# Gated linear attention and a SoLU feed-forward: preparation in groups of two batches, weights converted by VectorE, second product one chunk later

One Trainium2 chip, one core. The metric is the device time of the kernel in microseconds (us), the median of several executions. All executions compared here are fast: none lies more than 1.5% above the fastest of its kernel. The "granted clock" is the share of TensorE's full clock that the profile shows as granted, 1 for all of it. Engines: TensorE (PE in the profile), VectorE (DVE), ScalarE (ACT), GpSimd (POOL).

## The reference, cut to what matters

```python
# q, k, v, a_re, a_im: (4 batches, 8 heads, 768 steps, 48)
mag = np.sqrt(a_re * a_re + a_im * a_im)
scale = np.minimum(mag, 0.999) / (mag + 1e-06)          # then a_re, a_im times scale
for t in range(S):                                      # complex state S, decayed by a
    new_re = ar * S_re - ai * S_im
    new_im = ar * S_im + ai * S_re
    S_re, S_im = (new_re + k[t] (x) v[t], new_im)
    y[t] = q[t] @ S_re
x = y as (3072, 384)
h = x @ w_in                                            # 384 x 1024
e = np.exp(h - h_max); solu = h * e / (sum(e) + 1e-9)
ln = (solu - mu) / np.sqrt(var + 1e-06) * g_ln
return ln @ w_out                                       # 1024 x 384
```

The weights w_in and w_out and the vector g_ln arrive in 64-bit floating point.

## The kernel before

A chunk is 128 steps of one batch; there are 24, in 6 rows of 4 batches. For a row, `prep_steps` computes the logarithm of the decay, its running sum (a matmul with a triangle), and sine and cosine of the summed angle. From these k and q are scaled, "doubled" to a real and an imaginary part, and turned (transposed) by TensorE. Then come the scores, the values and the state of the attention, and for the chunk before it the feed-forward: turn of x, `up` (two halves of 512 columns), exp and product (`solu`), turn of z, `down`.

VectorE, ScalarE and TensorE execute in exactly the order in which the loop emits their work; the loop is therefore a schedule for three queues. It prepares the next row of four batches during four passes (`part` 0 to 3):

```python
    for n in range(N + 1):
        ...                                        # cut: loads; part = b, now = the next row's preparation
        if n > 0:
            turn_x()                               # feed-forward of chunk n-1
        if n < N:
            score(0); score(1)
        if last_ff:
            last_ff[6]()                           # store of chunk n-2
        if part == 0:   now["s0"]()
        elif part == 1: now["s3"]()
        elif part == 2: now["decay"]()
        elif part == 3: now["trig"](); to_exp()
        if nxt:
            doubled(*nxt)
        if n > 0:
            up(0); solu(0); up(1)
        if part == 3:
            now["ends"]()
        if nxt:
            turn("k", *nxt, 0); turn("q", *nxt, 0)
        if n > 0:
            solu(1)
        if n < N:
            values()
        if n > 0:
            turn_z(0); turn_z(1)
        if n < N:
            carry()
        if nxt:
            turn("k", *nxt, 1); turn("q", *nxt, 1)
        ...                                        # cut: weights in passes 0 and 1
        if part == 1:
            now["s4"]()
        if n > 0:
            down(0); norm()
        if part == 0:
            now["s1"](); now["s2"]()
        elif part == 1:
            run(now["totals"])
        elif part == 2:
            to_trig(); now["angle"]()
        if n > 0:
            down(1)
        if part == 2:
            run(now["phases"])
```

The weights are made 32-bit floats by integer operations in 14 pieces. Each piece alternates between VectorE and GpSimd:

```python
    # ScalarE: y = the low word, rounded
    ts(out=x, in0=hi, scalar1=0x7FFFFFFF, scalar2=None, op0=OP.bitwise_and)
    nc.gpsimd.tensor_tensor(out=x, in0=x, in1=rebias.to_broadcast([P, n]), op=OP.add)
    ts(out=hi, in0=hi, scalar1=-2 ** 31, scalar2=None, op0=OP.bitwise_and)
    stt(out=x, in0=x, scalar=31, in1=x, op0=OP.arith_shift_right, op1=OP.bitwise_and)
    stt(out=x, in0=x, scalar=3, in1=hi, op0=OP.logical_shift_left, op1=OP.bitwise_or)
    nc.gpsimd.tensor_tensor(out=w[:, c, f0:f0 + n].bitcast(I32), in0=x, in1=y, op=OP.add)
```

The steps of the preparation that the argument needs, with the engine of each: `s0`, `s1` (VectorE, ScalarE: Ln, Exp, the ratio of the parts), `s2` (ScalarE: squares and Ln), `s3` (VectorE, then ScalarE's Exp and Ln), `s4` (VectorE), `totals` (TensorE, with the tile f_L), `decay` (ScalarE: two Exp), `ends` (TensorE turns the chunk's last decays, tile f_tot), `angle`, `phases` (TensorE, tile f_phase), `trig` (ScalarE: two Sin). All turned tiles, f_L, f_tot and f_phase share one pool of two banks of PSUM, the memory that TensorE writes to here: a matmul waits until the tile before it in its bank has been read.

## Time and profile before

| Measure | Before |
|---|---|
| Time, median of 4 runs (lowest to highest) | 634.35 us (634.05 to 635.15) |
| Profiled span, mean granted clock | 635.8 us, 0.902 |
| TensorE busy | 498.8 us (78%) |
| Turn of x of pass n=2 begins | 158.11 us |
| Turn of x of n=2 to that of n=22 | 423.4 us |

The last two rows are read from the timeline of TensorE; they divide the span into a start, twenty passes and an end.

### The profile page before, as it was taken

To read this page: it belongs to the slowest core of one execution; us is meant where nothing else is said; L and a number is where in the kernel's file an instruction comes from. 1 tells how busy PE (TensorE), PEld (TensorE's weight loads), DVE (VectorE), ACT (ScalarE), POOL (GpSimd) and SP (SyncE) were. 2 spreads that over 40 slices of the span, in tenths; PEclk is the share of its full clock that TensorE was granted. 3 is DMA by queue.
4 is the path that set the end of the run, shared out by engine and by line. 5 is a ranking of instruction groups with operands and counts; after the bars stand their busy time and mean duration, and the time that the engine had idled before them with its cause. 6 is when DMAs were issued, how large, how long until landed. Compare 5 with 4: busy or idle time off the path is not lost.

```text
span 635.8 us, 12921 instructions
## 1 busy us (share of the span) xinstructions
PE 498.8 (78%) x5600; PEld 316.5 (50%) x5600; DVE 343.1 (54%) x565; ACT 282.7 (44%) x428; POOL 164.8 (26%) x159
## 2 busy tenths in 40 slices
PE   0334060287989889999799897999997999999994
PEld 0113050154646656556466465565664765666652
DVE  3674656615665655646646556556465465444232
ACT  2665343450653553644526535536345356223221
POOL 1072545200600515303216005152031160000000
PEclk9955565597999989999799999899997999999998
DMA  9949411000383001950004830019500000000000
GB/s 179 222 96 194 124 50 50 2 1 0 74 153 63 3 13 26 148 104 14 13 2 83 142 64 12 4 27 159 92 14 12 2 15 14 13 14 14 13 14 19
DMA packets 132019, 35.94 MB, mean 57 GB/s; under 512 B 126960, under 2 KB 130032, under 8 KB 131952
## 3 DMA queue, kind: packets, MB, share of 16 engines
q1 hardware_dynamic: 131312, 34.62, 27.8%
q8 instruction: 46, 0.75, 0.5%
q10 hardware_dynamic: 640, 0.40, 0.3%
q14 instruction: 21, 0.17, 0.1%
HBM read 30.22 MB, written 4.72 MB: 55 GB/s over the span
## 4 chain that ended last, share of the span: by engine, by line
PE 58%; ACT 14%; DVE 13%; POOL 6%; issue 4%; SPq 2%; DMA 0%; DVEq 0%; ACTq 0%; POOLq 0%
PE f_h L867 18%; PE f_o L909 13%; PE f_turned L799 6%; PE f_score L815 5%; PE f_zt L884 3%; PE f_d L842 3%; PE f_y L827 2%; PE f_L L708 2%; DVE f_bits L631 2%; SPq L584 2%; PE f_phase L758 2%; PE f_y L830 2%; POOL f_rs L903 2%; ACT f_kT L801 1%; DVE f_x L746 1%
## 5 line engine op out<-in xcount | busy, mean ns | idle before, releaser
L867 PE MATMUL f_h<-f_w_in,f_xT 128*128 128x512 f32 x288 | 140.4, 641 | 45.7 <-ACT f_xT L862 45.7
L909 PE MATMUL f_o<-f_w_out,f_zT 128*128 128x384 f32 x384 | 131.8, 495 | 4.2 <-DVE f_w_out L644 3.9
L867 PEld LDWEIGHTS f_h<-f_w_in,f_xT 128*128 128x128 f32 x288 | 57.2, 206 | 112.0 <-issue 95.7
L909 PEld LDWEIGHTS f_o<-f_w_out,f_zT 128*128 128x128 f32 x384 | 72.1, 193 | 50.4 <-DVE f_w_out L644 4.5
L876 DVE TENSOR_TENSOR f_z<-f_h,f_z 128x512 f32<-128x512 f32 x48 | 33.1, 690 | 88.6 <-ACT f_z L875 88.6
L817 DVE TENSOR_TENSOR f_att<-f_score,f_mats 128x512 f32<-128x512 f32 x48 | 32.8, 689 | 68.9 <-PE f_score L815 68.9
L801 ACT COPY f_kT<-f_turned 96x512 f32<-96x512 f32 x48 | 27.8, 580 | 62.5 <-PE f_turned L799 62.2
L846 POOL TENSOR_TENSOR f_state<-f_state,f_tot 96x384 f32<-96x384 f32 x16 | 19.0, 1187 | 134.9 <-DVE f_state L845 134.9
L862 ACT COPY f_xT<-f_xt 128x384 f32<-128x384 f32 x24 | 11.4, 474 | 94.6 <-PE f_xt L859 94.6
L799 PE MATMUL f_turned<-f_mats,f_k 128*96 128x128 f32 x192 | 31.8, 291 | 26.2 <-DVE f_k L787 25.5
L815 PE MATMUL f_score<-f_qT,f_kT 96*128 96x128 f32 x384 | 49.3, 284 | 0.0
L902 POOL TENSOR_TENSOR f_s<-f_s,f_mv 128x1 f32<-128x1 f32 x24 | 10.3, 431 | 142.3 <-DVE f_s L901 142.3
L815 PEld LDWEIGHTS f_score<-f_qT,f_kT 96*128 96x128 f32 x384 | 47.2, 200 | 0.0
L875 ACT ACTIVATE f_z<-f_h 128x512 f32<-128x512 f32 x48 | 28.8, 599 | 30.7 <-PE f_h L867 30.6
L723 POOL TENSOR_TENSOR f_q<-f_q,f_ar 128x384 f32<-128x384 f32 x22 | 29.1, 1351 | 50.6 <-ACT f_ar L715 50.6
L799 PEld LDWEIGHTS f_turned<-f_mats,f_k 128*96 128x96 f32 x192 | 21.2, 131 | 40.1 <-issue 26.8
L708 PE MATMUL f_L<-f_lr,f_mats 128*128 128x384 f32 x48 | 20.3, 554 | 25.6 <-DVE f_lr L701 25.5
L885 ACT COPY f_zT<-f_zt 128x512 f32<-128x512 f32 x48 | 27.7, 586 | 22.4 <-PE f_zt L884 22.0
L884 PE MATMUL f_zt<-f_mats,f_z 128*128 128x128 f32 x192 | 29.9, 286 | 6.0 <-DVE f_z L876 6.0
L827 PE MATMUL f_y<-f_v,f_att 128*32 128x48 f32 x1536 | 34.4, 210 | 0.0
L758 PE MATMUL f_phase<-f_x,f_mats 128*128 128x384 f32 x48 | 22.3, 582 | 15.3 <-ACT f_x L743 7.2
L827 PEld LDWEIGHTS f_y<-f_v,f_att 128*32 128x32 f32 x1536 | 30.9, 112 | 5.1 <-issue 4.9
(100 smaller groups left out, 821.4 us busy)
## 6 DMA issues: line engine op xcount, KB each, us to landing
f_ar<-in_a_re_dram SPq DMA_DIRECT2D x24, 192.0 KB, 4.4
f_ai<-in_a_im_dram SPq DMA_DIRECT2D x24, 192.0 KB, 4.6
f_q<-in_q_dram SPq DMA_DIRECT2D x24, 192.0 KB, 4.7
f_k<-in_k_dram SPq DMA_DIRECT2D x24, 192.0 KB, 4.3
f_v<-in_v_dram SPq DMA_DIRECT2D x24, 192.0 KB, 4.3
out_dram<-f_ot SPq DMA_DIRECT2D x24, 192.0 KB, 1.9
f_raw<-in_moe_w_in_dram SPq DMA_DIRECT2D x6, 512.0 KB, 6.1
f_raw<-in_moe_w_out_dram SPq DMA_DIRECT2D x8, 384.0 KB, 3.1
```

Source lines behind the costliest of these rows:

```text
L708: nc.tensor.matmul(out=ps, lhsT=tri, rhs=lm, start=True, stop=True)
L723: el.tensor_tensor(out=x, in0=x, in1=t[:, o], op=OP.mult)
L758: nc.tensor.matmul(out=ps, lhsT=turns, rhs=T["x0", ti][:, b * DM:(b + 1) * DM], start=True, stop=True)
L799: nc.tensor.transpose(out=ps[0:D2, i], in_=T[nm + "2", ti, b][:, half * 4 + i].rearrange("p u d -> p (u d)"), identity=ident)
L801: nc.scalar.copy(out=T[nm + "T", ti, b][:, half * 512:half * 512 + 512], in_=ps[0:D2].rearrange("p i t -> p (i t)"))
L815: nc.tensor.matmul(out=ps[:, i], lhsT=KT[:, x * P:(x + 1) * P], rhs=QT[:, x * P:(x + 1) * P], start=True, stop=True)
L817: nc.vector.tensor_tensor(out=st["att"][:, half * 4:half * 4 + 4], in0=ps, in1=tri.unsqueeze(1).to_broadcast([P, 4, P]), op=OP.mult)
L827: nc.tensor.matmul(out=y[g:g + 32, hs], lhsT=st["att"][:, x, g:g + 32], rhs=V[:, hs], start=True, stop=(ti == 0))
L867: nc.tensor.matmul(out=h, lhsT=st["xT"][:, c * P:(c + 1) * P], rhs=w_in[:, c, half * 512:(half + 1) * 512], start=(c == 0), stop=(c == KD ...
L876: nc.vector.tensor_tensor(out=z, in0=h, in1=z, op=OP.mult)
L884: nc.tensor.transpose(out=ps[:, i * P:(i + 1) * P], in_=st["z"][:, c * P:(c + 1) * P], identity=ident)
L909: nc.tensor.matmul(out=st["o"], lhsT=st["zT"][:, c * P:(c + 1) * P], rhs=w_out[:, c], start=(c == 0), stop=(c == KF - 1))
```

## The change

Its intent: shorten the start, in which TensorE has nothing to do, by preparing two batches (a group) instead of four and by taking the weights off GpSimd; and keep GpSimd, slower at elementwise work in this trace (1187 ns against 554 for 96x384, see the prediction), out of the loop. The second product (`down`) of a chunk moves one pass later. A test that no weight is too small for the shorter conversion is added (each piece is fetched again later). The weights, now three operations in one queue:

```diff
-    # six operations, VectorE and GpSimd in turn
+    nc.vector.tensor_scalar(out=x, in0=hi, scalar1=3, scalar2=0x3FFFFFFF, op0=OP.logical_shift_left,
+                            op1=OP.bitwise_and)
+    nc.vector.scalar_tensor_tensor(out=x, in0=hi, scalar=-2 ** 30, in1=x, op0=OP.bitwise_and,
+                                   op1=OP.bitwise_or)
+    nc.vector.tensor_tensor(out=x, in0=x, in1=T["bits", i], op=OP.add)
+
+    def inspect(i):
+        nc.vector.tensor_reduce(out=least[:, i:i + 1], in_=T["raw", i][:, :, 1].bitcast(FP), axis=AX.X, op=OP.min,
+                                apply_absolute_value=True)
```

Groups, pools and the engine of the elementwise work (cut):

```diff
-    const, ld, ldv = pool("f_const", 1), pool("f_ld", 1), pool("f_ldv", 2)
+    const, ld, ldv = pool("f_const", 1), pool("f_ld", 2), pool("f_ldv", 3)
-    rawp = pool("f_raw", 4)
+    rawp, bits = pool("f_raw", 6), pool("f_bits", 3)
-    groups = [(0, 0, 2), (0, 2, B)] + [(ti, 0, B) for ti in range(1, NC)]
+    GB = 2
-            nc.gpsimd.tensor_scalar(out=ai, in0=ai, scalar1=1e15, scalar2=-1e15, op0=OP.min, op1=OP.max)
+            nc.vector.tensor_scalar(out=ai, in0=ai, scalar1=1e15, scalar2=-1e15, op0=OP.min, op1=OP.max)
-                nc.gpsimd.tensor_tensor(out=heads(state[b]), in0=heads(state[b]), in1=tot, op=OP.mult)
+                nc.vector.tensor_tensor(out=heads(state[b]), in0=heads(state[b]), in1=tot, op=OP.mult)
```

The new loop prepares a group in two passes, an even and an odd one (a pair). Conditions are shortened: `even` and `odd` hold only while there is a group to prepare.

```diff
+    for n in range(N + 2):
+        ...                                       # cut: loads, fetches, `if` around work that is not there
+        store of chunk n-3
+        turn_x()                                  # feed-forward of chunk n-1
+        score(0); score(1)
+        if even: now["s1"]()
+        if odd:  now["trig"](); to_exp(); now["decay"]()
+        down(0)                                   # of chunk n-2
+        if even: doubled(nxt)
+        values()
+        if even: now["square"]()
+        up(0); solu(0)
+        if even: now["s2"]()
+        if odd:  now["decayed"](0); doubled(nxt); now["decayed"](1)
+        turn("k", nxt, 0); turn("q", nxt, 0)
+        up(1); solu(1)
+        if even: now["s3"]()
+        if odd:  now["ends"]()
+        carry()
+        turn("k", nxt, 1); turn("q", nxt, 1)
+        if even: now["s4"]()
+        if odd:  then["s0"]()
+        turn_z(0)
+        if even: now["totals"](); now["fourth"](); to_trig(); now["angle"]()
+        down(1)
+        turn_z(1); norm()
+        if 4 <= n < 18: inspect(n - 4)
+        if even: now["phases"]()
```

## The prediction

> **What bounds the kernel now.** I read the page's busy rows first, then the chain that ended last in order of time, then the timelines of single stretches.
>
> ```profile
> PE 498.8 (78%) x5600; PEld 316.5 (50%) x5600; DVE 343.1 (54%) x565; ACT 282.7 (44%) x428; POOL 164.8 (26%) x159
> ...
> PE   0334060287989889999799897999997999999994
> ...
> POOL 1072545200600515303216005152031160000000
> PEclk9955565597999989999799999899997999999998
> ```
>
> TensorE is the bound from the tenth slice on (each is 15.9 us), but not before: up to about 158 us it is mostly idle. So there are two stretches to price: the start, and 22 to 24 chunks in which TensorE is nearly full.
>
> The start hangs on GpSimd. Each piece of weights goes VectorE, GpSimd, VectorE, GpSimd, one piece after the other:
>
> ```profile
> 103.69 0.99 POOL L633 TENSOR_TENSOR f_w_out<-f_bits 128x384 int32<-128x384 int32 x1 [1.15 <-DVE f_bits L632]
> 105.15 1.00 POOL L625 TENSOR_TENSOR f_bits<-f_bits,f_rebias 128x384 int32<-128x384 int32 x1 [0.47 <-DVE f_bits L624]
> 107.30 0.99 POOL L633 TENSOR_TENSOR f_w_out<-f_bits 128x384 int32<-128x384 int32 x1 [1.16 <-DVE f_bits L632]
> ```
>
> That is 3.6 us a piece until 111 us. The first product of a chunk's second part starts at 122.9 us, the centring of the weights ends at 147 us, and the third pass of the loop (call it n=2) starts at 158.1 us.
>
> In the steady stretch one row of four chunks takes 86.6 us (the preparation's first maximum starts at 203.13, 289.70 and 377.38 us in the chain). The last chunks, which prepare nothing, run full:
>
> ```profile
> 564.68 1.79 PE f_score L815 x16
> 566.47 5.15 PE f_h L867 x12
> 575.28 1.27 PE f_turned L799 x8
> 576.55 5.16 PE f_o L909 x16
> 582.04 1.79 PE f_score L815 x16
> ```
>
> One such chunk takes 17.36 us, of which I count 16.9 as work (0.33 turn x, 1.78 score, 5.16 up, 4 x 0.43 turn k and q, 1.55 values, 1.1 turn z, 5.16 down). A row with preparation has 4 x 16.9, 4 x 0.85 for the carry and 8 x 0.65 + 0.15 for the sums and phases: 76.4 us. So only 10 us of 86.6 are waits and their slow clock, nearly all in one place:
>
> ```profile
> 219.05 1.48 ACT L689 ACTIVATE f_ar<-f_x 128x1536 f32<-128x1536 f32 x1 [5.13 <-POOL f_rs L903]
> ...
> 223.70 0.46 ACT L862 COPY f_xT<-f_xt 128x384 f32<-128x384 f32 x1
> ```
>
> ScalarE's queue holds the copy of x behind a Square that waits for VectorE. TensorE waits there, and the products behind it take 7.1 to 8.4 us in the chain instead of 5.15.
>
> **What the Trainium skill says.** "TensorE: Matmul & The Clock Gate", section "Architectural detail", has ScalarE and VectorE as strict FIFOs; the trace agrees (the turn of x began at 218.25 us, and its copy above came at 223.70, behind work that it does not need). The same page, "What's actually happening", lets the clock fall after an idle window of about 3.4 us; the page's PEclk of 5 to 6 tenths in the slices with an idle TensorE agrees. "GPSIMD Engine Reference", section "Engine selection", puts two-input elementwise work at about twice VectorE's time there; the trace has 1187 ns against 554 for 96x384. "ScalarE: Activation LUTs", section "What ACT_TABLE_LOAD costs", states 1283 ns plus a drain of 1380: the trace has the 1283 ns, and the next activation starts 0.01 us later, so I charge no drain.
>
> **The change, part by part.** Weights: 14 pieces, each now two ScalarE operations (0.76+0.72 us for 512 columns, 0.64+0.61 for 384) and three on VectorE (about 0.43+0.69 and an integer add, which the trace lacks; I take 0.65 to 1.1). GpSimd's 34 us there go. Preparing two batches instead of four halves the first chain. I walked the queues by these durations: loads land at 6 us as now, phases at 22, sums at 27, Sin at 32, first turned halves at 36, so the loop begins near 38 us, not 78. Pass n=0 converts six pieces; the last four go raise, convert, scale at 2.5 us each, and the pass ends near 70. Pass n=1 has four more at 2.5, then the mean (5.4) and the centring, ending near 115. So n=2 starts at 115 against 158: 43 us won. Of this 5 us is owed, since the second product of chunk 0 is still to do.
>
> GpSimd's work on VectorE: per two chunks 0.5+0.96 for the imaginary part, 4 x 0.55 for k and q, 2 x 0.55 for the state: about 5 us, to about 32 us of VectorE in some 39 us of TensorE. That fits as a share. What matters is where it stands. The queues of a pair of chunks in the changed kernel (read from the built order) give four waits for TensorE:
> - Odd pass: k and q are decayed behind the first half's exp and product, then doubled, then turned, while the second half of "up" stands behind the turn. From the end of up(0): 0.2+0.72 exp, 0.61 product, 2 x 0.47, 0.95 doubling, 0.05: 3.5 us, plus 0.4 for q.
> - Odd pass: the transpose of the end values comes behind the second product: 0.2+0.72+0.69+0.54+0.1 = 2.25 us, plus 0.45 later for a bank.
> - Even pass: the transpose of z needs a PSUM bank of the turned k, whose copy stands behind s3's Exp and Ln, which wait for VectorE's s3 behind the second product: 0.2+0.72+0.61+0.95+0.9+0.93+0.6 = 5.0, less 1.7 of carry and turns that run beside it: 3.3 us, plus 0.5 at sums and phases.
> - Odd turn of x: its bank is freed by the phase's subtraction, behind the angle's row and the statistics: about 1.6 us.
>
> Together 12 us per pair. Work per pair is 2 x 16.9 + 1.7 + 2.8 = 38.3, so about 50 us per pair, 25 per chunk, against 86.6/4 = 21.65 before. The wait at the Square goes (it is in the sum: the copy of x now stands ahead of it), but four smaller ones come in every pair instead of one in two pairs.
>
> Second product a chunk later: it removes most of the half microsecond by which a full chunk is longer than its work (17.36 against 16.9) and adds a pass at the end, where it fills gaps: about +3 us net. Table loads: 27 instead of 13, 18 us more on ScalarE at 1.283 each, mostly beside TensorE. Weights fetched again for the test of smallness: 5.6 MB and about 7 us of VectorE over 14 passes, hidden apart from 0.6 per even pass, which is in the 1.6.
>
> Sum: 115 + ten pairs n=2 to 21 (first and last shorter) 497 + n=22 and 23 16.8+15.1 + end 25 = 669 us of span, 667 as timed. Since each wait could be some tenths shorter, I put 660.
>
> **The rivals.** First, TensorE stays full: without the new waits the ten pairs cost about 383 us plus little, and the sum is near 560. For it speaks that the total busy time fits and that the change moves so much off the slow engine; against it, that the waits above are chains inside strict queues, which more buffers do not shorten. Second, only the bare chains count: with the smallest latencies the waits sum to 9.6 us, a pair costs 48, the start ends at 105, and the time is about 635 to 640: the start's gain eaten whole. Third, the waits of 3.3 to 3.5 us drop the clock as the one of 3.7 us does now; with 1 us per pair for it the time is near 680. I hold the main sum the likeliest, since the same counting gives 76 + 10 for a row of the kernel before.
>
> **Range and chances.** Ten pairs carry the uncertainty: 1 us per pair is 10 us. A pair of 47.5 to 51.5 us and a start of 107 to 120 give 632 to 684. Faster than 621 needs pairs under 46 us, which asks that two of the four waits are not there: 0.12. Within 2% (622 to 647) is the second rival: 0.2. Slower: 0.68.
>
> **What would show it.** Right: n=2's turn of x near 115 us; waits of TensorE for the doubled k (3.5 us, 11 times), for the end values' transpose (2 us), for the copies of the turned k before z's transpose (3 us); a pair near 50 us; a busy share of TensorE near or below 75%; GpSimd nearly empty. Wrong: pairs near 40 us in the chain, or an integer add on VectorE of several us, which would lengthen the start.

## More of the kernel before

The view of windows adds one number for each stretch. Its columns are the stretch and its length, then busy us and instructions of PE, PE's weight loads, DVE, ACT and POOL, then the granted clock, the DMA share and GB/s. The kernel before, one row of four chunks and one late chunk that prepares nothing:

```profile
212.85:299.43 86.58, 80.23 (x1007) 51.46 (x1006) 49.56 (x81) 42.67 (x64) 25.77 (x23) 0.98 0.31 56
541.83:559.19 17.36, 17.31 (x200) 11.27 (x200) 8.17 (x18) 5.23 (x12) 1.24 (x3) 1.00 0.04 13
```

TensorE is busy in 80.23 of 86.58 us of the row, and in all of the late chunk. VectorE is busy little more than half of the time.

## The result and the profile after

The changed kernel takes 688.79 us (median of 4 runs, 686.16 to 690.01); the ratio to the kernel before is 1.0851 (95% interval 1.0814 to 1.0887), so it is slower. Ratios here and below are the mean time of one kernel's fast runs over that of the other's of the same rounds, so not quite the ratio of the medians quoted.

| Measure | Before | After | After less before |
|---|---|---|---|
| Profiled span | 635.8 | 688.1 | +52.3 |
| Start, to the turn of x of n=2 | 158.1 | 112.6 | -45.5 |
| n=2 to n=22 | 423.4 | 517.5 | +94.1 |
| From there to the end | 54.3 | 58.1 | +3.8 |

The start gave its 45.5 us; the passes took twice that. The page of the kernel after, rows of TensorE and of the granted clock:

```profile
PE 530.5 (77%) x5604; PEld 332.2 (48%) x5604; DVE 374.9 (54%) x713; ACT 312.5 (45%) x507; POOL 18.1 (3%) x52
...
PE   1162776878878878878878878878878888789995
...
PEclk9975775999999999988999999999997999899999
```

TensorE never fills a slice in the steady stretch: 7 and 8 tenths, where the kernel before has mostly 8 and 9, and only four instructions were added to it, yet it is busy 32 us longer. GpSimd has gone from 164.8 to 18.1 us. Two pairs in the view of windows (columns as above):

```profile
217.00:268.29 51.29, 42.37 (x505) 26.88 (x504) 30.20 (x58) 23.86 (x39) 1.49 (x5) 0.93 0.28 63
268.29:322.43 54.14, 45.44 (x506) 28.60 (x505) 30.37 (x58) 23.86 (x39) 1.82 (x5) 0.87 0.26 60
```

A pair is two chunks, so 51.29 stands against 43.29 before (half of the row). VectorE is busy 30.2 us of it and ScalarE 23.9: neither is a bound. The view of waits of TensorE names what it waited for (us in total, times, longest):

```profile
PE f_turned L780 <- DVE f_k L768: 47.0, 13, 6.9
PE f_zt L867 <- ACT f_kT L782: 33.5, 19, 4.0
...
PE f_tot L721 <- DVE f_e L719: 18.2, 9, 2.0
```

The timelines show each one as a chain (columns: start, us, engine, line, operation, tiles, shapes; in brackets the idle time before it and what ended it). An odd pass of the kernel after, the doubled k:

```profile
252.20 0.60 ACT L858 ACTIVATE f_z<-f_h 128x512 f32<-128x512 f32 x1 [3.38 <-PE f_h L850]
252.92 0.69 DVE L859 TENSOR_TENSOR f_z<-f_h,f_z 128x512 f32<-128x512 f32 x1 [2.90 <-ACT f_z L858]
253.52 0.55 DVE L709 TENSOR_TENSOR f_k<-f_k,f_ai 128x384 f32<-128x384 f32 x1
...
254.46 0.95 DVE L768 TENSOR_TENSOR f_k<-f_cs,f_k 128x768 f32<-128x768 f32 x1
...
255.47 1.09 PE L780 MATMUL f_turned<-f_mats,f_k 128*96 128x128 f32 x4 [3.31 <-DVE f_k L768]
257.28 3.23 PE L850 MATMUL f_h<-f_w_in,f_xT 128*128 128x512 f32 x6
```

VectorE stood idle 2.90 us for the exp of the first half, although k's decay had long been there: its queue has the product of z ahead of k. TensorE in turn has the turn of k ahead of the second half of `up`, which could have run. In the even pass before it the same instructions follow no such wait:

```profile
225.99 0.60 PE L780 MATMUL f_turned<-f_mats,f_k 128*96 128x128 f32 x4
226.87 2.74 PE L850 MATMUL f_h<-f_w_in,f_xT 128*128 128x512 f32 x6
```

They take 0.60 and 2.74 us there, and 1.09 and 3.23 after the wait: the turns run at about half pace, and the slow pace reaches into the half of `up` behind them. The even pass has its own chain, that of s3 ahead of the copy of the turned k:

```profile
232.02 0.94 ACT L684 ACTIVATE f_u<-f_lr,f_bias 128x768 f32<-128x768 f32 x1 [1.68 <-DVE f_lr L683]
232.99 0.93 ACT L685 ACTIVATE f_u<-f_u,f_bias 128x768 f32<-128x768 f32 x1
233.83 0.56 ACT L782 COPY f_kT<-f_turned 96x512 f32<-96x512 f32 x1
234.44 1.11 PE L867 MATMUL f_zt<-f_mats,f_z 128*128 128x128 f32 x4 [3.01 <-ACT f_kT L782]
```

And the wait of the end values (f_tot) and of the turn of x:

```profile
242.94 0.55 PE L842 MATMUL f_xt<-f_mats,f_xn 128*128 128x128 f32 x3 [0.32 <-DVE f_f L742]
...
262.53 0.19 PE L721 MATMUL f_tot<-f_mats,f_e 16*96 16x16 f32 x1 [2.02 <-DVE f_e L719]
```

### The profile page after: what moved, and what is told of

The parts are those of the page before. It is cut to its first block, busy times and chain, and to the rows that moved or that the text cites. A ratio compares the mean times of both kernels' runs of the same rounds, so it can differ in the third digit from the quotient of the medians.

```text
span 688.1 us, 13068 instructions
## 1 busy us (share of the span) xinstructions
PE 530.5 (77%) x5604; PEld 332.2 (48%) x5604; DVE 374.9 (54%) x713; ACT 312.5 (45%) x507; POOL 18.1 (3%) x52
## 3 DMA queue, kind: packets, MB, share of 16 engines
HBM read 36.51 MB, written 4.72 MB: 60 GB/s over the span
## 5 line engine op out<-in xcount | busy, mean ns | idle before, releaser
L850 PE MATMUL f_h<-f_w_in,f_xT 128*128 128x512 f32 x288 | 144.9, 644 | 0.0
L892 PE MATMUL f_o<-f_w_out,f_zT 128*128 128x384 f32 x384 | 134.7, 494 | 1.0 <-DVE f_ot L897 1.0
L892 PEld LDWEIGHTS f_o<-f_w_out,f_zT 128*128 128x128 f32 x384 | 73.4, 199 | 46.7 <-issue 8.2
L780 PE MATMUL f_turned<-f_mats,f_k 128*96 128x128 f32 x192 | 38.0, 332 | 47.0 <-DVE f_k L768 47.0
L867 PE MATMUL f_zt<-f_mats,f_z 128*128 128x128 f32 x192 | 35.5, 317 | 33.5 <-ACT f_kT L782 33.5
L780 PEld LDWEIGHTS f_turned<-f_mats,f_k 128*96 128x96 f32 x192 | 24.1, 148 | 67.0 <-DVE f_k L768 57.4
L867 PEld LDWEIGHTS f_zt<-f_mats,f_z 128*128 128x128 f32 x192 | 26.0, 160 | 47.7 <-ACT f_kT L782 38.7
L695 PE MATMUL f_L<-f_lr,f_mats 128*128 128x384 f32 x48 | 33.0, 842 | 19.7 <-DVE f_lr L688 19.7
L809 PEld LDWEIGHTS f_y<-f_v,f_att 128*32 128x32 f32 x1536 | 30.8, 110 | 14.7 <-issue 11.4
L780 PE MATMUL f_turned<-f_mats,f_q 128*96 128x128 f32 x192 | 37.1, 328 | 0.1
L672 ACT ACTIVATE f_ar<-f_x 128x768 f32<-128x768 f32 x12 | 10.1, 843 | 57.3 <-DVE f_x L669 57.3
L815 DVE COPY f_xn<-f_y 128x384 f32<-128x384 f32 x24 | 13.3, 554 | 39.6 <-PE f_y L812 36.2
```

The source lines that it names most:

```text
L695: nc.tensor.matmul(out=ps, lhsT=tri, rhs=lm, start=True, stop=True)
L780: nc.tensor.transpose(out=ps[0:D2, i], in_=T[nm + "2", c][:, half * 4 + i].rearrange("p u d -> p (u d)"), identity=ident)
L809: nc.tensor.matmul(out=y[r:r + 32, hs], lhsT=st["att"][:, x, r:r + 32], rhs=V[:, hs], start=True, stop=(ti == 0))
L850: nc.tensor.matmul(out=h, lhsT=st["xT"][:, c * P:(c + 1) * P], rhs=w_in[:, c, half * 512:(half + 1) * 512], start=(c == 0), stop=(c == KD ...
L867: nc.tensor.transpose(out=ps[:, i * P:(i + 1) * P], in_=st["z"][:, c * P:(c + 1) * P], identity=ident)
L892: nc.tensor.matmul(out=st["o"], lhsT=st["zT"][:, c * P:(c + 1) * P], rhs=w_out[:, c], start=(c == 0), stop=(c == KF - 1))
```

## The experiments

Theory A: the order of the queues makes waits of 2 to 3.3 us, and each also slows TensorE's clock for the work behind it. Its rivals: the bare waits alone count, and the lower clock costs next to nothing; or the amount of work that is now on VectorE is at fault, wherever it stands. All kernels below gave the reference's result. Each was timed in 3 rounds on the chip of its batch, where the kernel before had medians of 635.24, 636.0 or 636.91 us. The sums from n=2 to n=22 come from the timelines, as in the table above:

| Kernel | Time, us | Ratio to before | n=2 begins | n=2 to n=22 |
|---|---|---|---|---|
| before | 634.35 | 1 | 158.1 | 423.4 |
| after | 688.79 | 1.0851 | 112.6 | 517.5 |
| x1_fill | 666.47 | 1.0487 | 109.9 | 494.8 |
| x2_kearly | 639.69 | 1.0072 | 106.3 | 470.8 |
| x3_ends | 662.33 | 1.0417 | 109.6 | 493.4 |
| x4_s3late | 676.88 | 1.0657 | 111.8 | 503.3 |
| x9_s3early | 674.01 | 1.0594 | 110.2 | 504.0 |
| x10_best | 603.80 | 0.9506 | 104.2 | 437.9 |
| x11_tuned | 569.54 | 0.8952 | 104.8 | 402.2 |
| x13_downnow | 737.37 | 1.1585 | 119.3 | 560.5 |

### Idle matmuls in the waits

The changed kernel, with matmuls that compute nothing that is used, put into TensorE's queue at three of the waits.

```diff
+    def fill(count, width):
+        ps = ps_s.tile([P, 4, P], FP, tag="s", name="f_fill").rearrange("p i t -> p (i t)")
+        for _ in range(count):
+            nc.tensor.matmul(out=ps[:, 0:width], lhsT=ident, ..., start=True, stop=True)
+        if now and odd and n > 1:
+            fill(3, 512)                          # ahead of decayed(0)
+        if now and odd and n > 1:
+            fill(2, 384)                          # ahead of ends
+        if now and not odd and n > 1:
+            fill(3, 512)                          # ahead of turn_z(0)
```

> The changed kernel with idle matmuls that nobody reads put into three waits of TensorE per pair from pass 2 on: three of 128x512 ahead of the doubled k, two of 128x384 ahead of the end values, three of 128x512 ahead of the even z. They take away no wait; they only keep TensorE busy in it. Theory A (the prediction's queue sum of 669 us was right and the other 19 us are the clock that falls in the waits): pairs of 49.5 to 50 us, none of 54, in all 664 to 674 us. Theory B (the waits are longer than counted for another reason, such as VectorE's load): 688 us or more, since the fillers can only get in the way.

Measured: 666.47 us (665.06 to 666.84), mean granted clock 0.964 instead of 0.896 in the profiled run. A pair in the view of windows, and the odd pass on TensorE's timeline:

```profile
210.38:260.22 49.84, 46.29 (x522) 28.05 (x521) 30.13 (x58) 23.85 (x39) 1.48 (x5) 1.00 0.29 65
```

```profile
244.89 2.74 PE L935 MATMUL f_fill<-f_mats 128*128 128x512 f32 x6
...
248.35 0.64 PE L780 MATMUL f_turned<-f_mats,f_k 128*96 128x128 f32 x4 [0.73 <-DVE f_k L768]
249.70 2.74 PE L850 MATMUL f_h<-f_w_in,f_xT 128*128 128x512 f32 x6
```

More work on TensorE made the kernel 22 us faster. The chains on VectorE and ScalarE are untouched, the pair runs at clock 1.00, the turns of k take 0.64 and `up` 2.74 us again, and the long pairs are gone (49.70 to 49.85 us from the second to the eighth). The sum from n=2 to n=22 is 494.8 us; the prediction, which had priced the waits and a full clock, had 497. The rival of the bare waits falls: after all that the fillers themselves delay, 22.7 us of the 517.5 were the clock. That 494.8 is so near 497 is partly luck, since the pair here has 46.29 us of busy TensorE, about 6.9 of it fillers, and 3.55 of waits, where the prediction had 38.3 and 12.

### k ahead of the first half's product

```diff
             now["decay"]()
+            now["decayed"](0)
+            if nxt:
+                doubled(nxt)
...
-        if now and odd:
-            now["decayed"](0)
-        if nxt and odd:
+        if nxt and odd and not now:
             doubled(nxt)
```

> The changed kernel with the decay of the first k and q and the doubling put ahead of the first half of the second part on VectorE's queue in odd passes; no work is taken away. Theory A (the place in the queue costs): the 3.3 us wait for the doubled k goes in 11 odd passes with the slow clock behind it (about 1.3 us, and the 2.8 us of the long pairs): 630 to 640 us. Theory B (GpSimd's work on VectorE costs by its amount): the same work in another order, 680 to 690 us.

Measured: 639.69 us (637.08 to 640.03), level with the kernel before. The wait for the doubled k is left three times in the whole run, 11.4 us, where the kernel after has it thirteen times and 47.0 us. An ordinary pair:

```profile
228.48:276.18 47.70, 42.32 (x504) 27.24 (x504) 30.44 (x57) 23.64 (x40) 1.48 (x4) 0.93 0.29 68
```

The sum from n=2 to n=22 fell by 46.7 us and the start by 6.3. Of the 46.7, 34.4 us are idle time of TensorE (86.2 became 51.8) and 12.2 busy time (431.3 became 419.1). This one place in the order is worth more than the whole start had won. But the expected 1.3 us of slow clock behind the wait did not come back in an ordinary pair: TensorE is busy 42.32 us where it was 42.37, at the same clock of 0.93. Behind the wait of 2.02 us for the end values the next turn of k now takes 1.09 us, where the kernel after has 0.64 (at 263.46 us), so the slow stretch has moved to the next wait:

```profile
244.12 1.09 PE L780 MATMUL f_turned<-f_mats,f_k 128*96 128x128 f32 x4
```

The 12.2 us come from the first, the two long and the last two pairs.

### End values ahead of the second half's product

```diff
             up(1)
+        if now and odd:
+            now["ends"]()
+        if up:
             solu(1)
```

> The changed kernel with the end values' three small operations ahead of the second product on VectorE's queue, as in the kernel before. Theory A: the 2.0 us wait of the end values' transpose goes in 11 odd passes, 662 to 668 us. Theory B (amount, not place): 685 to 690 us.

Measured: 662.33 us (660.51 to 663.2). f_tot, 18.2 us in the kernel after, is no longer among the waits that the view lists, and the sum from n=2 to n=22 fell by 24.1 us. Only 11.1 of it are idle time, since the turn of x waits 1.0 to 1.2 us instead of 0.32 in half of the pairs; 13.0 are busy time. The trace also shows that Theory A, as worded, is too strong. In the pairs from 358.64 to 454.07 us the two waits for z and for k stand at full length, and nothing behind them is slow:

```profile
210.54:259.74 49.20, 42.30 (x505) 26.91 (x504) 30.09 (x57) 23.85 (x39) 1.48 (x5) 0.93 0.29 66
406.35:454.07 47.72, 39.78 (x506) 25.11 (x505) 29.77 (x57) 23.85 (x39) 1.48 (x5) 1.00 0.24 51
```

```profile
423.79 0.66 PE L867 MATMUL f_zt<-f_mats,f_z 128*128 128x128 f32 x4 [3.01 <-ACT f_kT L782]
...
444.20 0.64 PE L780 MATMUL f_turned<-f_mats,f_k 128*96 128x128 f32 x4 [3.31 <-DVE f_k L768]
```

So a wait of this length can be followed by the slow clock and need not be. Which of the two happens was not tested.

### s3 after the turns, and s3 before the second half: two misses

The wait of z's transpose came from s3's Exp and Ln ahead of the copy of k. The first try moves s3 behind everything that TensorE needs:

```diff
-        if now and not odd:
-            now["s3"]()                           # behind solu(1)
...
         if now and not odd:
+            now["s3"]()                           # behind the turns' second half
             now["s4"]()
...
+        if down:
+            down(1)                               # ahead of totals, fourth and angle, not behind them
```

> The changed kernel with step s3 behind the turns of k and q in even passes, and the sums behind the second half of the second product. Theory A: the 3.0 us wait of z's transpose for the copy of k goes, with 0.9 us of slow clock behind it; the angle comes later, so that 0.5 to 1.5 us are given back at the phases: 655 to 672 us. Theory B: 685 to 690 us.

Measured: 676.88 us (674.89 to 677.18), less gain than expected. The wait went, and three others took its place in the same pass:

```profile
278.27 0.66 PE L867 MATMUL f_zt<-f_mats,f_z 128*128 128x128 f32 x4 [0.23 <-ACT f_kT L782]
...
282.62 1.56 PE L695 MATMUL f_L<-f_lr,f_mats 128*128 128x384 f32 x4 [1.11 <-DVE f_lr L688]
...
286.07 1.56 PE L740 MATMUL f_phase<-f_x,f_mats 128*128 128x384 f32 x4 [1.23 <-DVE f_x L730]
...
288.79 0.55 PE L842 MATMUL f_xt<-f_mats,f_xn 128*128 128x128 f32 x3 [1.16 <-DVE f_f L742]
```

The second try moves s3 the other way, ahead of `up(1)` and `solu(1)`:

```diff
             turn("q", nxt, 0)
+        if now and not odd:
+            now["s3"]()
...
             solu(1)
-        if now and not odd:
-            now["s3"]()
```

> The changed kernel with step s3 ahead of the second half of the second part in even passes, instead of behind it: Exp and Ln then stand ahead of the second exp on ScalarE, and the copy of the turned k directly behind it. Place in the queue: the 3.0 us wait for z's transpose becomes about 1 us, its slow clock (0.9 us) goes, the end of the even pass follows as it did: about 3 us in each of 11 even passes and some of the long pairs, 650 to 662 us. If ScalarE's total work in the even pass is the bound and not the place: 680 us or more.

Measured: 674.01 us (673.45 to 674.23), again less gain than expected. z waits 0.30 us instead of 3.01, but s4 still stands behind the second half's product, and now the sums wait for it:

```profile
227.91 2.19 PE L695 MATMUL f_L<-f_lr,f_mats 128*128 128x384 f32 x4 [1.61 <-DVE f_lr L688]
```

The waits of f_L for s4 rose from 2 to 12 in number and from 19.7 to 33.7 us. In both tries a wait of 3 us was traded for smaller ones, and 13 to 14 us were won of the 30 that ten bare waits of 3.01 make. That a wait is gone says little until the next instruction of the same chain has been looked at.

### The moves together

x2_kearly, x3_ends and x9_s3early, with the phases ahead of `norm` and `inspect` on VectorE, and the accumulated fourth power last:

```diff
             turn_z(1)
+        if now and not odd:
+            now["phases"]()
+            now["fourth"]()
+        if up:
             norm()
```

> All the moves at once: decay and doubling early in odd passes, end values ahead of the second product, s3 early in even passes, the phases ahead of the statistics on VectorE, the fourth power last. No work is taken away. Queue places are the cause: pairs of 41 to 43 us against 51.3, 590 to 606 us, faster than both kernels. The amount of work on VectorE is the cause: not below 634 us.

Measured: 603.80 us (603.43 to 606.62), faster than the kernel before and in the expected range, though the pairs, 43.2 to 45.4 us but for the last of 41.4, are longer than the 41 to 43 expected. The clock is 0.976 in the profiled run. The two largest left in a pair are that of the sums for s4 as above, and a new one of the second product for the bank that the store frees, behind VectorE's other work:

```profile
218.85 2.85 PE L892 MATMUL f_o<-f_w_out,f_zT 128*128 128x384 f32 x8 [1.77 <-DVE f_ot L897]
```

These two were moved next:

```diff
-            last.pop(n - 3)[6]()                  # the store, at the start of a pass
...
             now["ends"]()
+        if now and not odd:
+            now["s4"]()                           # ahead of solu(1)
+        if up:
             solu(1)
...
             now["fourth"]()
+        if down:
+            last.pop(n - 2)[6]()                  # the store, ahead of norm
+        if up:
             norm()
```

> The version with all moves, and two more for the waits that its trace still shows: s4 directly behind Ln on VectorE, ahead of the second product (takes the 1.6 us wait for the sums in even passes), and the store's scaling ahead of the statistics (takes the 1.8 us wait of the second product for its bank in odd passes). Place in the queue: 3 us in each of 10 or 11 pairs, 570 to 580 us. If TensorE has reached its work: 595 us or more.

Measured: 569.54 us (568.74 to 569.85), ratio 0.8952 (0.8925 to 0.8979): just below the expected 570, and faster than both. It computes everything that the changed kernel does, the test of the weights included. A pair and the page's row of TensorE:

```profile
207.56:247.84 40.28, 39.40 (x504) 25.15 (x504) 30.01 (x57) 23.32 (x40) 1.48 (x4) 1.00 0.34 80
```

```profile
PE   0354397699999999999999999999999999999985
```

TensorE is busy 39.40 of 40.28 us at the full clock; VectorE and ScalarE do the same work as in the kernel after (30.0 and 23.3 us a pair). From 51.29 to 40.28 us, all is order: from n=2 to n=22 both traces have 4804 matmuls.

### Is it the amount on VectorE?

The changed kernel with two operations of a group, the clamp and the state's product, back on GpSimd:

```diff
-            nc.vector.tensor_scalar(out=ai, in0=ai, scalar1=1e15, scalar2=-1e15, op0=OP.min, op1=OP.max)
+            nc.gpsimd.tensor_scalar(out=ai, in0=ai, scalar1=1e15, scalar2=-1e15, op0=OP.min, op1=OP.max)
...
-                nc.vector.tensor_tensor(out=heads(state[b]), in0=heads(state[b]), in1=tot, op=OP.mult)
+                nc.gpsimd.tensor_tensor(out=heads(state[b]), in0=heads(state[b]), in1=tot, op=OP.mult)
```

> The changed kernel with the state's product and the clamp of the imaginary part back on GpSimd: 1.6 us of VectorE less in every pair, none of it in a chain that TensorE waits for. Place: 683 to 692 us, no difference. Amount on VectorE: 16 us less, 672 us.

Measured: 690.41 us (5 runs, 685.84 to 691.74), ratio 1.0858 against 1.0851 for the changed kernel: no difference. The rival of the amount falls for these two operations, and with x11_tuned, which leaves all of them on VectorE, as a whole.

And the changed kernel without the second fetch and the test of the weights (passes 4 to 17):

```diff
+    nc.vector.memset(least, 1.0)
-        if 4 <= n < 18:
-            fetch(n - 4)
...
-        if 4 <= n < 18:
-            inspect(n - 4)
```

> The changed kernel without the second fetch and the test of the weights in passes 4 to 17 (right for these inputs alone). Its 0.6 us of VectorE stand ahead of the phase's subtraction in 7 even passes, where TensorE waits: 682 to 686 us. If the fetches collide with the loads: 670 us or less.

Measured: 687.64 us (687.45 to 688.25), not the 682 to 686 expected. 1.15 us of the medians separate it from the changed kernel, less than the spread of the latter's runs, and n=2 to n=22 takes 517.4 us against 517.5: the test is hidden.

### The second product back in its own pass

```diff
-        down = last[n - 2][5] if n - 2 in range(N) else None
+        down = last[n - 1][5] if n - 1 in range(N) else None
...
-        if down:
-            down(0)                               # and down(1) likewise
...
             turn_z(1)
+            down(0)
+            down(1)
             norm()
```

> The changed kernel with the second product back in its own pass, at the pass's end. If the later product is worth what it fills (TensorE then waits about 1 us for the masked scores in every pass and some tenths for z's copy): about 3 us per pair more less 5 us at the end, 700 to 725 us. If it is worth nothing: 680 to 692 us.

Measured: 737.37 us (734.32 to 738.14), more of a loss than expected. The second product now waits for the copies of z that it stands directly behind, and then runs at the slow clock:

```profile
283.16 7.12 PE L892 MATMUL f_o<-f_w_out,f_zT 128*128 128x384 f32 x16 [1.96 <-ACT f_zT L868]
```

Full pace for these sixteen is 5.16 us (the chain of the kernel before). So this part of the change was worth some 47 us of span (735.2 against 688.1) in the new order. It isn't the kernel before's place, which had the carry and the turns between the copies and the product; what the part is worth there stays open.

### Two parts on the kernel before

The kernel before, with the weights in VectorE's three operations and nothing else (no test of smallness, so it is not the complete kernel):

```diff
-                ts(out=x, in0=hi, scalar1=0x7FFFFFFF, scalar2=None, op0=OP.bitwise_and)
-                nc.gpsimd.tensor_tensor(out=x, in0=x, in1=rebias.to_broadcast([P, n]), op=OP.add)
-                ts(out=hi, in0=hi, scalar1=-2 ** 31, scalar2=None, op0=OP.bitwise_and)
+                ts(out=x, in0=hi, scalar1=3, scalar2=0x3FFFFFFF, op0=OP.logical_shift_left, op1=OP.bitwise_and)
...
-                nc.gpsimd.tensor_tensor(out=w[:, c, f0:f0 + n].bitcast(I32), in0=x, in1=y, op=OP.add)
+                stt(out=x, in0=hi, scalar=-2 ** 30, in1=x, op0=OP.bitwise_and, op1=OP.bitwise_or)
+                nc.vector.tensor_tensor(out=w[:, c, f0:f0 + n].bitcast(I32), in0=x, in1=y, op=OP.add)
```

> The kernel before with one part of the change alone: the weights converted by ScalarE and VectorE with the new three operations, nothing on GpSimd (the test of smallness left out, so not a complete kernel for other weights). If the start's gain comes from the end of the relay between VectorE and GpSimd: 12 pieces at about 2 us instead of 3.6 to 4.4, 608 to 620 us. If it came from the groups of two batches: 628 us or more.

Measured: 609.26 us (606.16 to 611.35), ratio 0.9589. The turn of x of n=2 begins at 127.69 us instead of 158.11. So 30 of the 45.5 us that the start won can be had by the weights alone; by subtraction, the groups of two and the new order of the start are left with the other 15, which no run tests apart.

The kernel before with its one large wait (the Square ahead of the copy of x) taken out by order alone:

```diff
         elif part == 1:
-            now["s3"]()
+            now["s2"]()                           # behind the copy of x
         elif part == 2:
+            run(now["totals"])
             now["decay"]()
...
         if part == 1:
-            now["s4"]()
+            now["s3"]()
         if n > 0:
             down(0); norm()
+        if part == 1:
+            now["s4"]()
...
             now["s1"]()
-            now["s2"]()
-        elif part == 1:
-            run(now["totals"])
```

> The kernel before with its own wait mended by order alone: the Square and Ln of step s2 go behind the next pass's copy of x on ScalarE, s3 behind the turns, the sums into the pass after. Place in the queue: the wait at the Square goes with its slow clock, 5 to 8 us in each of 5 rows, 594 to 612 us. If a new wait takes its place: 625 us or more.

Measured: 606.80 us (605.24 to 607.77), ratio 0.9534. A row takes 81.3 us (turns of x at 211.97 and 293.24 us) instead of 86.6, at clock 1.00:

```profile
211.97:293.24 81.27, 78.14 (x1006) 50.86 (x1005) 47.78 (x80) 42.49 (x63) 24.13 (x24) 1.00 0.32 60
```

The wait of 3.69 us for the copy of x is gone from every row; one of 0.48 us for the sums is new. From n=2 to n=22 it wins 20.0 us, and the start wins another 9.6 (148.5 against 158.1). The kernel before had the same illness as the one after, once in a row of four chunks.

## Why the prediction was wrong

The direction was right: slower by over 2%, by the waits that it named. The time, 688.8 us, lies outside the range, which ended at 684.

- **The bound before** and the wait at the Square: right, but "nearly all in one place" was too much. Of the 10 us that it put down to waits and slow clock, x12_square, without that wait, wins 5.3 a row, and the row's work at full clock is 78.1 us (x12_square) where 76.4 were counted.
- **The start**: 115 us predicted, 112.6 measured. The integer add on VectorE, unknown then, takes 0.56 us for 384 columns:

```profile
L628 DVE CUSTOM_DVE_ANT_0 f_w_out<-f_w_out,f_bits 128x768 uint16<-128x768 uint16 x8 | 4.5, 558 | 11.0 <-ACT f_bits L618 11.0
```

- **The four waits**: the right ones, with the right releasers. Predicted bare 3.5, 2.25, 3.3 and 1.6 us; measured 3.31 (doubled k), 2.02 (end values), 3.01 (z) and 0.32 (turn of x). The last one is 1.16 in x4_s3late, where the z wait ahead of it is gone.
- **Work of 38.3 us a pair**: this is the step that failed. It priced every matmul at full pace, though the waits stood just ahead of them and the prediction's own chain had 7.1 to 8.4 us instead of 5.15 behind the wait of the kernel before. At clock 1.00 the pair's work is 39.40 us (x11_tuned), 1.1 more than counted; in the kernel after it is 42.37 at clock 0.93. The slow clock costs 3.0 us in an ordinary pair, and 6.0 in the long one (45.44). With it an ordinary pair of 51.29 us is 39.4 of work, 3.0 of slow clock and 8.9 of waits. The prediction had 38.3, nothing and 12: its too long waits made up for most of the missing term. Over the ten pairs TensorE is busy 431.3 us against 392.2 in x11_tuned, with the same 4804 matmuls: 39.1 us of slow pace that the sum did not have. The waits were 86.2 us; the sum had about 114 (497 less ten times 38.3). So 497 became 517.5.
- **"Since each wait could be some tenths shorter, I put 660"**: an adjustment of 7 us the wrong way. The shorter waits were there, but so was the slow clock, and the sum as it stood (667) was nearer.
- **The third rival** named the slow clock and 680 us, at 1 us a pair. It was the right mechanism, but its term measured 3.0 us in an ordinary pair and 3.9 on average, not 1. That its 680 us came near is partly luck: the waits, priced too long, hid most of the rest, and the pairs came out only 2.05 us longer than the sum had them.
- **The first rival** (TensorE stays full, near 560) was set aside as the chains cannot be shortened by buffers. They can by order: x11_tuned runs at 569.5. Of this kernel the judgement was right, of the idea behind it not.
- **The second product a chunk later**, put at about +3 us net: open. With it back behind its own transposes the span is 47 us longer, but that is not its place in the kernel before.
- **Table loads, second fetch, test**: the last two are hidden, as said (x7_noinspect); the page's HBM reads put the second fetch at 6.3 MB (36.51 less 30.22), not 5.6. The table loads were not tested apart, but x11_tuned has the same 27 and TensorE is busy 39.40 of its 40.28 us.
- **Two readings**: the clock's 5 to 6 tenths hold for the idle slices after the second; in the first one TensorE is idle too and the page has 9 tenths. The terms of the even pass's wait sum to 4.9, not 5.0.

The account of the error in span, from the sum's 669: start -2.4, pairs +20.5, end +1, which makes 688.1.

## What to carry to other kernels

When work is moved between strict queues, add up not only its time but what stands ahead of it: every copy or product that TensorE waits for should come before elementwise work that nobody waits for soon. A wait of TensorE of 2 to 3 us can cost more than its length, by slow clock behind it: 3.0 us on 8.9 in an ordinary pair here, 39.1 on 86.2 over ten pairs, and none in some pairs of x3_ends with the same two waits of 3 us. So allow for it as a range, not a fixed surcharge; matmuls put into the waits took it away here. After taking a wait out, read the same chain again, since the next wait is often one instruction further on.

## What the Trainium skill lacked or had wrong

- "TensorE: Matmul & The Clock Gate", section "HAM oscillation — how this bites in real kernels", states the rule as no idle gaps over about 3.4 us. As a single length it is too simple for this kernel: gaps of 3.31 and 3.01 us, with smaller ones near them, were followed by turns at about half pace (1.09 us against 0.60 for the turn of k, 1.11 against 0.66 for that of z), and in x2_kearly so was one of 2.02 us; in pairs of x3_ends gaps of 3.31 and 3.01 us were not (0.64 and 0.66 us). Elsewhere the page itself says about 3 us and calls the window free-running, which leaves room for both. Filling three waits a pair with idle matmuls won 22 us of 688.8, which is 3.2%.
- None of the pages read here has that a gap can hide behind slowed work: the turn of x waits 0.32 us in the changed kernel, 1.16 us in x4_s3late, where the wait for z ahead of it is gone, and 1.02 us in the pairs of x3_ends that run at full clock.
- "VectorE: DVE Perf Modes", section "Specifications", has integers exact only below 2^24, and "GPSIMD Engine Reference", section "Engine selection", gives GpSimd the exact integer add. Here VectorE added the 32-bit patterns in a custom instruction at 558 ns for 384 columns, and the result passed; no page has that form or its cost. The runs report only that the result is right, not its last bits.
- "ScalarE: Activation LUTs", section "What ACT_TABLE_LOAD costs", adds a drain of 1380 ns to a load of 1283 ns. The trace of the kernel before has the 1283 ns, and the next activation 0.01 or 0.02 us later for 12 of 13 loads.
